# The first MLP's float64 weight tiles: fetched ahead of the branch and narrowed by a queue through the prologue

## The chip, the cores and the metric

The kernel runs on one core of one Trainium2 chip. The time is the device time of one execution in microseconds (us), lower is better; the kernel before takes 721.33 us in the median of three runs (718.95 to 722.62). The core's engines each work through a queue of their own in order: TensorE (PE, with its weight loads as PEld), VectorE (DVE), ScalarE (ACT), GpSimd (POOL), and SyncE (SP), which here issues all DMA transfers.

## What is computed

Windowed attention with a few global columns feeds two MLPs, one after the other. Cut to what matters:

```python
# attention: q, k, v (2, 8, 768, 64); keep = global columns, or 0 <= row - col < n_local (96)
a = softmax(where(keep, q @ k.T / 8 + bias, -1e9))
x = (a @ v).transpose(0, 2, 1, 3).reshape(1536, 512)
# first MLP: w_in (512, 2048), w_out (2048, 512)
h = x @ w_in
x = (h * cos(h)) @ w_out
# second MLP: w_gate, w_val (512, 1536), w_out (1536, 512)
g = x @ w_gate
out = (g / (1 + exp(-g)) * (x @ w_val)) @ w_out
```

The weights arrive as float64 and are worked on as float32. Each float32 operand of a large product is split in a high and a low part, and three products (high-high, high-low, low-high) are added up.

## The kernel before

**The weights.** Each weight matrix is cut in tiles of 128 x 512 float64 values (512 KB): 16 of `w1i` and 16 of `w1o` for the first MLP, 36 for the second. `fetch` (L167) takes a staging buffer `st` from a pool of three, issues the transfer on SP (L174) and returns `narrow`, which turns the 64-bit words into float32 with three VectorE operations on 128 x 512 integers: L183 (mask and shift of the high word), L186 (sign and exponent) and L193 (bits of the low word). The text calls these three together a narrowing. The result `w` stays in SBUF for all blocks. A staging buffer is free for the third fetch after it only when its narrowing has read it.

**Before each use** a `w` is split: ACT rounds it to the high part (L206, `ws`), and DVE or POOL subtracts to get the low part (L210).

**The windowed path.** A flag computed from `n_global` and `n_local` picks a branch (L142, L1158); with the inputs given it is `windowed_path`. Its `prologue` (L972) does the attention of the first four tiles of 128 tokens in eight pairs of heads: scores on PE (L777, with a mask added by L789), maximum on DVE (L795, `mx`) and its negative (L799, `nm`), exponentials on ACT (L809, `sb`), the split of the probabilities on ACT (L861) and POOL or DVE (L862, `ph`), a transposing DMA on SP (L864, `pt<-ph`), the product with `v` (L890), and at the end of a tile its normalization (L903, `xn`), PE transposes (L220), and the split into `xh` on ACT (L225) and `xl` on DVE (L226). Rows of `v` are also summed in absolute value for a scale (`va` L662, `vsum` L663, `vm` L669 to `vsc` L679).

**The first MLP.** `first_mlp` (L246) goes over three blocks of 512 tokens, 16 steps each. Step s of a block makes `h` with 12 matmuls (L274), then k on ACT (L300), f on DVE (L311), sine and square on ACT (L320, L321), the product on DVE (L328), its split (L332 on ACT, L338 on DVE), and two steps later 12 matmuls into `y` (L350). The other eight attention tiles are worked into the steps of the first two blocks: tile by tile at the steps of `BASES`, with scores L753 and their masked maximum on DVE (L829). In the last block the code is in the order in which it is written; up to there a scheduler orders each engine's queue ahead of time. All narrowings of the first MLP lie in its first block: step s asks for `w1i` tile s+2 and `w1o` tile s+1 at its start and narrows `w1i` s+2 and `w1o` s behind its chain:

```python
            if s < NF1:
                get("i", s + 2)
                get("o", s + 1)
...
            if s < NF1:
                use("i", w_in, s + 2)
                use("o", w_out, s)
```

Only `begin` (called at pair 5 of the prologue) narrows ahead of the steps: `w1i` 0 and 1.

Of the kernel before, what the change touches and what calls it, by code (L numbers as in the profile page):

```python
# [15 lines left out]
I32 = mybir.dt.int32  # L16
# [6 lines left out]
P = 128  # L23
B, H, S, D = 2, 8, 768, 64
NTOK = B * S
DM = H * D
# [31 lines left out]
HB = 5  # L58
HE = 6
GVE = "DMMDDDDDDMDM"  # L60
M1E = "GDDGGDG"
# [8 lines left out]
def attention_moe_moe2_kernel(  # L70
# [15 lines left out]
    NF1 = w1i.shape[0]  # L86
# [9 lines left out]
    ws_p = ctx.enter_context(tc.tile_pool(name="ws", bufs=2))  # L96
    st_p = ctx.enter_context(tc.tile_pool(name="st", bufs=3))

# [68 lines left out]
    def fetch(src, j, pool=wr_p, tag="w"):  # L167

        if not wide:
            w = pool.tile([P, DM], F32, tag=tag, name="w")  # L170
            nc.sync.dma_start(out=w, in_=src[j])
            return lambda half=None: w
        t = st_p.tile([P, DM, 2], I32, tag="st", name="st")
        nc.sync.dma_start(out=t, in_=src[j].bitcast(I32).rearrange("p (n w) -> p n w", w=2))  # L174
# [23 lines left out]

        return narrow

    def eng(which, n):
        return nc.vector if n < len(which) and which[n] == "D" else nc.gpsimd
# [20 lines left out]
    def x_split(i, xT):  # L223
        cols = slice(i * P, (i + 1) * P)
        nc.scalar.copy(out=xh[:, :, cols], in_=xT)  # L225
        nc.vector.tensor_tensor(  # L226
            out=xl[:, :, cols], in0=xT, in1=f32(xh[:, :, cols]), op=ALU.subtract
        )
# [17 lines left out]
    def first_mlp(c1, before, steps, last_block):  # L246
        w_in, w_out = {}, {}
        got = {}
        todo = [(b, j) for b in range(len(BLOCKS)) for j in range(NF1)]
# [3 lines left out]

        def get(nm, j):
            if j < NF1 and (nm, j) not in got:
                got[nm, j] = fetch(w1i if nm == "i" else w1o, j)

        def use(nm, d, j):
            if j < NF1 and j not in d:
                d[j] = got.pop((nm, j))()  # L260

# [103 lines left out]
        def begin():  # L365
            get("i", 0)
            get("i", 1)
            get("o", 0)
            use("i", w_in, 0)
            use("i", w_in, 1)  # L370
            prep_in(0)

        before(hp, begin, prep_in, h_early)
        ch_p = c1.enter_context(tc.tile_pool(name="ch", bufs=2))
# [3 lines left out]
        for s in range(last):  # L378
            early, late = steps.get(s, ((), ()))
            if s < NF1:  # L380
                get("i", s + 2)
                get("o", s + 1)
            ps = h_mm(s)
            if s >= 2:
                y_mm(s - 2)
            prep_in(s + 1)
            if s >= 1:
                chain_b(s - 1)
            for th in early:
                th()  # L390
            if s >= 1:
                chain_c(s - 1)
                chain_d(s - 1)
            if s < NF1:
                use("i", w_in, s + 2)
                use("o", w_out, s)
            prep_out(s - 1)
            chain_a(s, ps)
            for th in late:
                th()  # L400
# [186 lines left out]
    def windowed_path():  # L587
# [7 lines left out]
        with ExitStack() as ca:  # L595
# [375 lines left out]

            def prologue(hp, begin, prep_in, h_early):  # L972
                with (
# [33 lines left out]
                    for w in range(NW + LAG + 2):  # L1007
# [24 lines left out]
                        if w >= 1 and w - 1 < NW:  # L1032
                            i, pp = pairs[w - 1]
                            for p in (2 * pp, 2 * pp + 1):
                                pools["p"] = (pph, ph_p)[pp]
                                split_p(i, p, eng(PLE, 4 * i + p), nc.scalar.copy)
                        if w == HB:
                            begin()
# [22 lines left out]
    def general_path():  # L1061
        half = TB // 2 * P
        with ExitStack() as cg:
# [19 lines left out]
            for b in range(B):  # L1083
# [6 lines left out]
                for t in range(TB):  # L1090
# [63 lines left out]
                    nc.vector.tensor_copy(out=xn, in_=x)  # L1154
                    x_split(i, x_turn(xn, ps_x, "xT"))
        moe(lambda hp, begin, *_: begin(), {}, lambda: None)

# [46 lines left out]
```

## Time and profile before

| | before |
|---|---|
| median of 3 runs | 721.33 us |
| profiled execution | 719.88 us, span 718.1 us |
| PE busy | 668.2 us (93%) |
| DVE busy | 484.5 us (67%) |
| ACT busy | 390.0 us (54%) |
| POOL busy | 112.3 us (16%) |
| TensorE clock granted, mean | 0.958 |

The profile is of one execution, taken by the hardware profiler. Its span is 1.8 us shorter than that execution's own time, and this execution is 1.45 us faster than the median of the runs. Shares of busy time are averages over stages that differ: the prologue, the first block with the narrowings, the second block, and the rest. PE's busy time is that of modelled ends, and it counts half-clock work at its length, so a busy PE is not PE at its peak. The clock column is the granted share of full speed; the two levels are 1.2 and 2.4 GHz.

### The profile page before, as it was taken

How to read it: one execution, taken by the hardware profiler on the slowest of the kernel's cores; microseconds unless marked ns; L12 is line 12 of the kernel's file. 1: busy time of each engine (PE TensorE's matmuls, PEld its weight loads, DVE VectorE, ACT ScalarE, POOL GpSimd, SP SyncE). 2: the span in 40 equal slices, each digit the busy share in tenths (PEclk: the TensorE clock that was granted, in tenths of full speed). 3: DMA queues.
4: the chain of work that ended last, by engine and by line, in shares of the span. 5: the costliest groups of instructions: out<-in, count | busy, mean ns of one | idle time of the engine just before them, and what ended most of it. 6: DMA issues, size and time to landing. Idle time of an engine off the chain costs nothing.

```text
span 718.1 us, 9055 instructions
## 1 busy us (share of the span) xinstructions
PE 668.2 (93%) x3276; PEld 525.9 (73%) x3276; DVE 484.5 (67%) x885; ACT 390.0 (54%) x816; POOL 112.3 (16%) x108
## 2 busy tenths in 40 slices
PE   4767986997998999999999999999999999999996
PEld 2446764775776777787888888888888888888884
DVE  3897899799988565747999779887544443434441
ACT  4675757578497887766666643333343333333331
POOL 2663323423222332420000000000000000000000
PEclk9776899798999999999999999999999999999998
DMA  6799656657552222300322224532100000100001
GB/s 216 184 205 230 166 138 206 137 152 193 147 117 60 40 40 45 60 1 30 112 93 89 88 59 135 158 118 88 38 22 0 1 1 0 59 0 1 1 0 63
DMA packets 69508, 62.73 MB, mean 87 GB/s; under 512 B 48880, under 2 KB 55024, under 8 KB 69456
## 3 DMA queue, kind: packets, MB, share of 16 engines
q1 hardware_dynamic: 69456, 62.08, 31.8%
q8 instruction: 27, 0.44, 0.3%
q14 instruction: 25, 0.20, 0.1%
HBM read 47.19 MB, written 3.15 MB: 70 GB/s over the span
## 4 chain that ended last, share of the span: by engine, by line
PE 77%; DVE 11%; DMA 6%; ACT 3%; issue 1%; POOL 0%; SPq 0%; DVEq 0%; ACTq 0%; POOLq 0%
PE h L274 15%; PE v L492 14%; PE g L492 14%; PE o L528 14%; PE y L350 14%; PE s L753 3%; DMA st<-w1i 2%; DVE w L186 2%; PE x L890 1%; PE s L777 1%; DVE w L193 1%; DMA pt<-ph 1%; DVE w L183 1%; DMA v<-v 1%; DVE h L328 1%
## 5 line engine op out<-in xcount | busy, mean ns | idle before, releaser
L210 DVE TENSOR_TENSOR ws<-w,ws 128x512 fp32r<-128x512 f32 x161 | 111.2, 711 | 93.8 <-ACT ws L206 93.6
L350 PE MATMUL y<-g,ws 128*128 128x512 f32 x576 | 145.1, 397 | 12.6 <-ACT g L332 11.0
L274 PE MATMUL h<-xh,ws 128*128 128x512 f32 (+1 forms) x392 | 137.4, 411 | 2.7 <-ACT xh L225 2.5
L350 PEld LDWEIGHTS y<-g,ws 128*128 128x128 f32 x576 | 108.6, 191 | 39.1 <-ACT g L332 12.9
L206 ACT CAST ws<-w 128x512 fp32r<-128x512 f32 x204 | 121.8, 616 | 21.8 <-DVE w L193 16.8
L528 PE MATMUL o<-ws,a 128*128 128x512 f32 x432 | 104.7, 391 | 0.0
L492 PE MATMUL v<-xh,ws 128*128 128x512 f32 x288 | 96.3, 395 | 0.0
L274 PEld LDWEIGHTS h<-xh,ws 128*128 128x128 f32 x392 | 77.9, 201 | 24.1 <-ACT xh L225 3.2
L492 PE MATMUL g<-xh,ws 128*128 128x512 f32 x288 | 94.7, 390 | 0.0
L528 PEld LDWEIGHTS o<-ws,a 128*128 128x128 f32 x432 | 81.1, 188 | 18.4
L274 PE MATMUL h<-xl,ws 128*128 128x512 f32 (+1 forms) x196 | 79.7, 407 | 3.3 <-DVE xl L226 3.3
L210 POOL TENSOR_TENSOR ws<-w,ws 128x512 fp32r<-128x512 f32 x43 | 58.6, 1363 | 134.6 <-ACT ws L206 126.6
L504 ACT ACTIVATE sl<-g 128x512 f32<-128x512 f32 x36 | 21.5, 598 | 97.5 <-PE g L492 97.5
L492 PEld LDWEIGHTS v<-xh,ws 128*128 128x128 f32 x288 | 54.2, 188 | 12.7
L492 PEld LDWEIGHTS g<-xh,ws 128*128 128x128 f32 x288 | 54.1, 188 | 11.2
L514 ACT CAST a<-sl 128x512 fp32r<-128x512 f32 x36 | 22.4, 623 | 72.5 <-DVE sl L510 72.5
L492 PE MATMUL v<-xl,ws 128*128 128x512 f32 x144 | 56.9, 395 | 0.0
L492 PE MATMUL g<-xl,ws 128*128 128x512 f32 x144 | 56.0, 389 | 0.0
L186 DVE SCALAR_TENSOR_TENSOR w<-st,w 128x512 int32<-128x512 int32 x68 | 51.0, 760 | 1.2
L193 DVE SCALAR_TENSOR_TENSOR w<-st,w 128x512 int32<-128x512 int32 x68 | 50.2, 746 | 0.8
L300 ACT ACTIVATE k<-h 128x512 int32<-128x512 f32 x48 | 28.5, 594 | 39.3 <-PE h L274 39.2
L274 PEld LDWEIGHTS h<-xl,ws 128*128 128x128 f32 x196 | 39.4, 201 | 12.4 <-DVE xl L226 4.0
(109 smaller groups left out, 822.2 us busy)
## 6 DMA issues: line engine op xcount, KB each, us to landing
st<-w1i SPq DMA_DIRECT2D x16, 512.0 KB, 3.9
st<-w1o SPq DMA_DIRECT2D x16, 512.0 KB, 4.4
st<-w2g SPq DMA_DIRECT2D x12, 512.0 KB, 3.8
st<-w2v SPq DMA_DIRECT2D x12, 512.0 KB, 3.7
st<-w2o SPq DMA_DIRECT2D x12, 512.0 KB, 3.8
vr<-v SPq DMA_DIRECT2D x16, 256.0 KB, 3.8
kr<-kT SPq DMA_DIRECT2D x12, 256.0 KB, 3.8
qr<-qT SPq DMA_DIRECT2D x12, 256.0 KB, 3.7
```

The lines of the kernel that those rows point to most:

```text
L186: nc.vector.scalar_tensor_tensor(out=w, in0=hi, scalar=-(1 << 30), in1=w, op0=ALU.bitwise_and, op1=ALU.bitwise_or,)
L193: nc.vector.scalar_tensor_tensor(out=w, in0=lo, scalar=29, in1=w, op0=ALU.logical_shift_right, op1=ALU.bitwise_or,)
L206: nc.scalar.copy(out=s[:, 0, :], in_=w)
L210: e.tensor_tensor(out=s[:, 1, :], in0=w, in1=f32(s[:, 0, :]), op=ALU.subtract)
L274: nc.tensor.matmul(hps[s][:, c0:c1], lhsT=wis[s][:, a, k * P:(k + 1) * P], rhs=xx[:, k, t0 + c0:t0 + c1], start=(k == 0 and a == 0 and xx ...
L300: nc.scalar.activation(out=k[:, :n], in_=ps[:, :n], func=AF.Copy, scale=INV2PI)
L350: nc.tensor.matmul(ys[b][m][:, :n], lhsT=w[:, a, m * P:(m + 1) * P], rhs=g[:, c, :n], start=(j == 0 and a == 0 and c == 0), stop=(j == NF1 ...
L492: nc.tensor.matmul(ps[:, :n], lhsT=w[:, a, k * P:(k + 1) * P], rhs=xx[:, k, t0:t0 + n], start=(k == 0 and a == 0 and xx is xh), stop=(k == ...
L504: nc.scalar.activation(out=sl[:, :n], in_=ps_.pop(("g", s))[:, :n], func=AF.Silu)
L514: nc.scalar.copy(out=a[:, 0, :n], in_=sl[:, :n])
L528: nc.tensor.matmul(os_[b][m], lhsT=a[:, c, m * P:(m + 1) * P], rhs=w[:, d, :], start=(j == 0 and c == 0 and d == 0), stop=(j == NF2 - 1 an ...
L753: nc.tensor.matmul(o, lhsT=qr[r, i % 3, c, :], rhs=k, start=True, stop=True)
```

## The change

The three staging buffers become one tile of three slots, `st[:, n % 3]`. An `order` list holds the 32 tiles as they will be narrowed (i0, i1, i2, o0, i3, o1, i4, o2, and so on), and `fetch_next` issues the next. Three are fetched before the branch. `conv1` narrows the oldest tile fetched and fetches one more. The prologue calls it at each of its rounds as often as `CV` says, 13 times in all; each step of the first block calls it twice more while tiles are left; `need` calls it for whatever a step lacks. The branch not taken fetches its own again.

```diff
+CV = (2, 2, 1, 1, 1, 1, 1, 1, 1, 1, 1)
...
-    st_p = ctx.enter_context(tc.tile_pool(name="st", bufs=3))
+    st_p = ctx.enter_context(tc.tile_pool(name="st", bufs=1))
+    st = st_p.tile([P, 3, DM, 2], I32, name="st")
+    taken = [0]
...
-        t = st_p.tile([P, DM, 2], I32, tag="st", name="st")
+        t = st[:, taken[0] % 3]
+        taken[0] += 1
...
+    order = [t for j in range(NF1 + 2) for t in (("i", j), ("o", j - 2)) if 0 <= t[1] < NF1]
+    every = list(order)
+    fetched = []
+
+    def fetch_next():
+        if order:
+            nm, j = order.pop(0)
+            fetched.append(((nm, j), fetch(w1i if nm == "i" else w1o, j)))
+
+    for _ in range(3):
+        fetch_next()
...
-        def get(nm, j):
-            if j < NF1 and (nm, j) not in got:
-                got[nm, j] = fetch(w1i if nm == "i" else w1o, j)
-
-        def use(nm, d, j):
-            if j < NF1 and j not in d:
-                d[j] = got.pop((nm, j))()
+        def conv1():
+
+            if fetched:
+                (nm, j), fn = fetched.pop(0)
+                (w_in if nm == "i" else w_out)[j] = fn()
+                fetch_next()
+
+        def need(s):
+
+            while (s + 2 < NF1 and s + 2 not in w_in) or (s < NF1 and s not in w_out):
+                conv1()
...
-            get("i", 0)
-            get("i", 1)
-            get("o", 0)
-            use("i", w_in, 0)
-            use("i", w_in, 1)
+            while 1 not in w_in:
+                conv1()
             prep_in(0)
...
-            if s < NF1:
-                get("i", s + 2)
-                get("o", s + 1)
...
-                use("i", w_in, s + 2)
-                use("o", w_out, s)
+                conv1()
+                conv1()
+                need(s)
...
+                        for _ in range(CV[w] if w < len(CV) else 0):
+                            conv1()
```

The lines of the kernel move down with it: the narrowing is L187, L190 and L197, the fetch L178, the prologue's `mx` L810, f L331. What the scheduler makes of it is seen at three places.

SP's queue at the start of the program, from the load of the first keys (`kr`) and queries (`qr`) through the flag and the branch to the first rows of `v`. Before:

```order
L110 DMA kr<-kT 128x4x128
L115 DMA qr<-qT 128x512
L142 TENSOR_LOAD flag_i
L142 ISA x2
L1158 COMPARE_AND_BRANCH
L110 DMA kr<-kT 128x4x128
L115 DMA qr<-qT 128x512
L998 DMA v_223<-v 128x2x512
```

With the change:

```order
L113 DMA kr<-kT 128x4x128
L118 DMA qr<-qT 128x512
L178 DMA st<-w1i 128x1024
L145 TENSOR_LOAD flag_i
L145 ISA x2
L178 DMA st<-w1i 128x1024 x2
L1179 COMPARE_AND_BRANCH
L113 DMA kr<-kT 128x4x128
L118 DMA qr<-qT 128x512
L1013 DMA v_227<-v 128x2x512
```

Two fetches now stand between the flag and the second load of keys, and a third ahead of the flag.

DVE's queue in the prologue, from the end of the first tile's sums (`r<-sum`) past the maxima of the second tile's two halves (`mx`). Before:

```order
L897 TENSOR_SCALAR r<-sum 128x8
L900 RECIPROCAL r<-r 128x8
L862 TENSOR_TENSOR ph<-sb,ph 128x256
L795 TENSOR_REDUCE mx<-s_313 128x4
L799 TENSOR_SCALAR nm<-mx 128x4
L183 TENSOR_SCALAR w<-st 128x512
L795 TENSOR_REDUCE mx<-s_368 128x4
L669 TENSOR_REDUCE vm<-vsum 128x8
L799 TENSOR_SCALAR nm<-mx 128x4
L186 SCALAR_TENSOR_TENSOR w<-st,w 128x512
L673 TENSOR_SCALAR vm<-vm 128x8
```

With the change:

```order
L912 TENSOR_SCALAR r<-sum 128x8
L915 RECIPROCAL r<-r 128x8
L877 TENSOR_TENSOR ph<-sb,ph 128x256
L810 TENSOR_REDUCE mx<-s_337 128x4
L187 TENSOR_SCALAR w<-st 128x512
L814 TENSOR_SCALAR nm<-mx 128x4
L190 SCALAR_TENSOR_TENSOR w<-st,w 128x512
L197 SCALAR_TENSOR_TENSOR w<-st,w 128x512
L187 TENSOR_SCALAR w<-st 128x512
L810 TENSOR_REDUCE mx<-s_397 128x4
L684 TENSOR_REDUCE vm<-vsum 128x8
L190 SCALAR_TENSOR_TENSOR w<-st,w 128x512
```

These are the fourth and fifth narrowings in the changed queue; three more stand ahead of the piece, where before there were none. Up to the f of step 0 the queue has 15 whole narrowings and one operation of the next (before: four and three operations), from there to the f of step 8 the rest of 32 (before: up to the 20th).

DVE's queue in the first MLP, from the f of step 8 to the f of step 9. Before:

```order
L311 SCALAR_TENSOR_TENSOR f<-h,k 128x512
L338 TENSOR_TENSOR g<-h,g 128x512
L183 TENSOR_SCALAR w<-st 128x512 x2
L186 SCALAR_TENSOR_TENSOR w<-st,w 128x512 x2
L193 SCALAR_TENSOR_TENSOR w<-st,w 128x512 x2
L903 TENSOR_TENSOR xn<-x,r 128x512
L210 TENSOR_TENSOR ws<-w,ws 128x512
L328 SCALAR_TENSOR_TENSOR h<-f,h 128x512
L311 SCALAR_TENSOR_TENSOR f<-h,k 128x512
```

With the change:

```order
L331 SCALAR_TENSOR_TENSOR f<-h,k 128x512
L918 TENSOR_TENSOR xn<-x,r 128x512
L358 TENSOR_TENSOR g<-h,g 128x512
L734 CAST vs<-vr 128x512
L912 TENSOR_SCALAR r<-sum 128x8
L915 RECIPROCAL r<-r 128x8
L916 TENSOR_TENSOR r<-r,vsc_143 128x8
L735 TENSOR_TENSOR vs<-vr,vs 128x512
L227 TENSOR_TENSOR ws<-w,ws 128x512
L348 SCALAR_TENSOR_TENSOR h<-f,h 128x512
L331 SCALAR_TENSOR_TENSOR f<-h,k 128x512
```

No narrowing of the first MLP is left there; the rows of attention (`vs`, `r`) have moved up.

## Rows read from the trace of the kernel before

**Rows 1.** The page's slices: 40 equal parts of the span, busy tenths, granted clock.

```profile
PE   4767986997998999999999999999999999999996
PEclk9776899798999999999999999999999999999998
```

**Rows 2.** Windows, four stages: busy us (instructions) per engine, clock, DMA share, GB/s.

```profile
0.00:72.80 72.80, 47.93 (x331) 31.56 (x332) 50.13 (x99) 42.99 (x134) 32.55 (x46) 0.80 0.83 207
72.80:144.10 71.30, 61.93 (x284) 45.68 (x282) 63.10 (x133) 47.23 (x101) 25.67 (x19) 0.87 0.58 164
144.10:211.40 67.30, 62.19 (x348) 47.54 (x347) 62.74 (x126) 49.88 (x115) 20.53 (x17) 0.95 0.56 157
211.40:274.00 62.60, 60.63 (x337) 45.24 (x336) 44.82 (x106) 51.03 (x110) 19.48 (x16) 1.00 0.29 53
```

**Rows 3.** Timeline, DVE: the f of steps 0 and 24.

```profile
72.77 0.69 DVE L311 SCALAR_TENSOR_TENSOR f<-h,k 128x512 f32<-128x512 f32 x1 [1.10 <-ACT k L300]
...
273.96 0.68 DVE L311 SCALAR_TENSOR_TENSOR f<-h,k 128x512 f32<-128x512 f32 x1
```

**Rows 4.** Windows of DVE work on `st` alone (the narrowings): busy us, instructions.

```profile
20.00:72.80 52.80, 8.23 (x15) 0.73 0.93 211
72.80:144.10 71.30, 31.57 (x45) 0.87 0.58 164
144.10:211.40 67.30, 27.29 (x36) 0.95 0.56 157
```

**Rows 5.** The chain that ended last, 0 to 110 us: start, us, what.

```profile
7.46 5.53 DMA v<-v
...
13.54 1.50 ACT sb L809 x8
...
43.31 0.06 DVE mx L795
...
91.74 2.05 DVE w L186 x2
```

**Rows 6.** Timeline, SP's queue: issues between the branch and the rows of v.

```profile
6.20 0.56 SPq L110 DMA_DIRECT2D kr<-kT  x1
...
11.43 0.67 SPq L174 DMA_DIRECT2D st<-w1i  x1
...
64.33 0.38 SPq L174 DMA_DIRECT2D st<-w1o  x1
```

**Rows 7.** Windows, all engines: three stretches of the prologue.

```profile
6.00:20.00 14.00, 9.60 (x41) 5.73 (x43) 5.94 (x21) 8.26 (x33) 1.94 (x5) 1.00 0.70 243
20.00:72.80 52.80, 38.33 (x292) 25.83 (x291) 43.06 (x72) 33.00 (x100) 28.66 (x24) 0.73 0.93 211
13.00:17.00 4.00, 2.71 (x8) 1.11 (x8) 0.00 (x0) 3.59 (x16) 0.00 (x0) 1.00 1.05 401
```

**Rows 8.** Timeline, DVE: its two longest waits in the prologue.

```profile
18.09 0.17 DVE L897 TENSOR_SCALAR r<-sum 128x8 f32<-128x8 f32 x1 [6.28 <-ACT sb L809]
...
65.81 0.41 DVE L736 COPY vs<-relt 32x1024 f16<-32x1024 f16 x1 [3.26 <-PE x L890]
```

**Rows 9.** Timeline, DVE: two narrowings side by side.

```profile
82.38 0.76 DVE L183 TENSOR_SCALAR w<-st 128x512 int32<-128x512 int32 x2
...
83.76 1.29 DVE L186 SCALAR_TENSOR_TENSOR w<-st,w 128x512 int32<-128x512 int32 x2
84.97 1.29 DVE L193 SCALAR_TENSOR_TENSOR w<-st,w 128x512 int32<-128x512 int32 x2
```

**Rows 10.** Timeline, POOL and DVE: the same operations while POOL works.

```profile
88.07 3.05 POOL L210 TENSOR_TENSOR ws<-w,ws 128x512 fp32r<-128x512 f32 x2 [6.09 <-ACT ws L206]
...
89.88 1.86 DVE L183 TENSOR_SCALAR w<-st 128x512 int32<-128x512 int32 x2
91.66 2.13 DVE L186 SCALAR_TENSOR_TENSOR w<-st,w 128x512 int32<-128x512 int32 x2
```

**Rows 11.** Timeline, DVE: its longest wait from step 0 to 8.

```profile
138.27 0.29 DVE L829 CUSTOM_DVE_ANT_0 sb<-s,m 128x128 f32<-128x128 f32 x1 [3.18 <-PE s L753]
```

More of the change, by code (lines that the diff above doesn't have):

```diff
@@ L247, in first_mlp @@
         w_in, w_out = {}, {}
-        got = {}
         todo = [(b, j) for b in range(len(BLOCKS)) for j in range(NF1)]
@@ L365, in begin @@
         def begin():
-            get("i", 0)
-            get("i", 1)
-            get("o", 0)
-            use("i", w_in, 0)
-            use("i", w_in, 1)
+            while 1 not in w_in:
+                conv1()
             prep_in(0)
-        before(hp, begin, prep_in, h_early)
+        before(hp, begin, prep_in, h_early, conv1)
         ch_p = c1.enter_context(tc.tile_pool(name="ch", bufs=2))
@@ L970, in windowed_path, with prologue @@
             }
-            def prologue(hp, begin, prep_in, h_early):
+            def prologue(hp, begin, prep_in, h_early, conv1):
                 with (
@@ L1155, in general_path @@
                     x_split(i, x_turn(xn, ps_x, "xT"))
+        del fetched[:]
+        order[:] = every
+        for _ in range(3):
+            fetch_next()
         moe(lambda hp, begin, *_: begin(), {}, lambda: None)
```

## The prediction

> **What bounds the kernel now.** I read the slices of the page first [rows 1]. From the 18th slice on PE is busy nine tenths or more at full clock; before that PE and its clock go up and down together. So only the first 211 us or so can move. I cut the time at the f operation of steps 0, 8, 16 and 24 of the first MLP (the first and the last of the four in [rows 3]) and took busy times per stage [rows 2]. The reader is to see three different limits.
>
> Up to step 0 (72.8 us) nothing is full: DVE is busy 50.1 us, PE 47.9. From step 0 to 8 (71.3 us) DVE is busy 63.1 us; PE's 61.9 us are worth 61.9 x 0.87 = 53.9 us at full clock. From step 8 to 16 (67.3 us) DVE is busy 62.7 us, PE 62.2 at a clock of 0.95, so 59.1 at full clock. DVE bounds both stages, PE close behind in the second. Then step 16 to 24, with no narrowing, takes 62.6 us, PE busy 60.6 at full clock: PE bounds it. The narrowings [rows 4] are 8.2 us of DVE work after 20 us in the prologue, 31.6 us in steps 0 to 8 and 27.3 us in steps 8 to 16. The chain that ended last agrees: in the steps it runs through the w operations, and in the prologue through loads, exponentials and, for some ten us from 43 us on, DVE's queue [rows 5].
>
> **The change, part by part.** No narrowing and no transfer is saved: 32 tiles before and after. It is only their place that moves. By the order of the queues, up to step 0 there are 11 whole narrowings more, and two single operations fewer in balance; from step 0 to 8 there are 16 and two operations (before 14 and three); from step 8 on none (before 12).
>
> *Price of a narrowing.* Two of them side by side: L183 0.76 us for both, L186 from 83.76 to 84.97, L193 much the same [rows 9]: 0.38 + 0.60 + 0.60 = 1.6 us each, with nothing else on the way. In the prologue before they cost 8.23 / 5 = 1.65 us, in the steps 2.1 (31.57 / 15) and 2.3 (27.29 / 12) [rows 4].
>
> *Start.* The first three narrowings (4.8 us) fall where DVE waited 6.28 us for the first exponentials [rows 8]: they cost nothing. If that wait were gone they would cost their 4.8 us. Two fetches are issued between the flag and the loads of keys, queries and the first rows of v. The chain goes through that load of v: issued at 7.46, it took 5.53 us, and ACT's exponentials start at 13.54 behind it [rows 5]. An issue takes SP 0.6 us [rows 6], so the load is at least 1.2 us later. One MB at the 401 GB/s at which the queue moved from 13 to 17 us [rows 7] is 2.6 us. Ends: 1.2, and 3.8 if they add. I take 2.6, since the issues run while the data move. The fetch ahead of the flag costs nothing: SP stood waiting for the flag there, until 6.2 us.
>
> *Rest of the prologue.* Eight more narrowings less 1.0 us for the single operations: 8 x 1.6 - 1.0 = 11.8 us on DVE. From 20 to 72.8 us DVE was busy 43.06 [rows 7], so 9.7 us were free. The longest piece, 3.26 us before the copy at 65.81 [rows 8], waits on PE's x and the transposes behind it, and by the order two narrowings stand there: it takes 3.3 us of them. Of the other 6.4 us, all short gaps, I take half, 3.2: a narrowing in front of a maximum fills a gap, and delays the maximum that ACT waits for by as much. 11.8 - 3.3 - 3.2 = 5.3 us. Ends: 2.1 (all gaps filled) and 11.8 (none). Prologue together: 2.6 + 5.3 = +7.9 us (3.3 to 15.6).
>
> *Steps 0 to 8.* Two narrowings more, less one operation: +2.6 us of DVE work; rows of attention move both ways, -0.4 in balance. DVE's free time there is 8.2 us; 3.18 us of it stand behind PE's scores at 138.27 [rows 11], in the stage with the lower granted clock of the two with narrowings (0.87 against 0.95 [rows 2]). I choose to count this gap as gone, since PE should have its weights earlier and wait less: 2.6 - 0.4 - 3.2 = -1.0 us. Ends: +2.2 (waits as before), and -6.0 (8.2 us of waits gone).
>
> *Steps 8 to 16.* Without 27.3 us of narrowings DVE needs some 35 us and cannot bound the stage. What bounds then is PE, as in steps 16 to 24: 62.6 us [rows 2]. 67.3 - 62.6 = -4.7 us. Ends: 0 (the chain of k, f, sine, g hangs as before) and -8.2 (PE's 59.1 us at full clock without a gap).
>
> *After step 16* PE bounds on both sides; the second MLP's narrowings and fetches stay where they are. 0.
>
> Sum: 7.9 - 1.0 - 4.7 = +2.2 us. The profiled execution took 719.9 us, so 722.1; it is 1.45 us under the median of the runs, which makes 723.5 us. The point of it: DVE's free time ahead of step 0 is bought with delay of the prologue, while the stage relieved, steps 8 to 16, has PE close behind DVE and gives back only 4.7 of the 27.3 us taken out.
>
> A rule of the Trainium skill speaks on the price. The rows first: while POOL subtracted (88.07 to 91.1), two L183 took 1.86 us and the two L186 after them 2.13 us, against 0.76 and 1.29 alone [rows 9, 10]. The Trainium skill, "SBUF — State Buffer", section "Who interferes with whom", says that a VectorE instruction with two SBUF inputs contends with a GpSimd instruction that reads SBUF, and that the loser fully blocks; the trace agrees in the growth shown. By that rule the prologue, POOL's busiest stage, would be the worst place for narrowings; by the row of the prologue's own (1.65 us each) it is not. It gives the second rival.
>
> **The rivals.**
>
> *The prologue swallows it (faster).* All gaps filled, 3.3 us there, -1.0 in steps 0 to 8, and PE at full clock in steps 8 to 16, -8.2: -5.9 us, 714.0, or 715.4 by the median. For it: 22.7 us of DVE idle ahead of step 0, and PE at 0.95 of its clock in the stage relieved. Against: the chain runs through DVE's queue for part of the prologue, where more work delays the end at once. Chance 0.24.
>
> *DVE and POOL in each other's way (slower).* POOL is busy 28.66 of 52.8 us in the prologue [rows 7], 20.5 of 67.3 in steps 8 to 16 [rows 2]. Beside POOL a narrowing costs (1.86 + 2.13 + 2.13) / 2 = 3.1 us in place of 1.6. Eight of them at POOL's share of 54%: 8 x 0.54 x 1.5 = +6.5 us over the sum, 730 us. Against it stand the 1.65 us of the prologue's own five. It decides from about two in eight on: then the time passes 724.9. Chance 0.18.
>
> *The queue of SP and the DMA engines (slower).* From 20 us to step 0 there would be 11 fetches in place of 6 (7 up to 64.33 us, the first at 11.43 [rows 6]; 16 by the order, 5 of them early). Each now waits for a narrowing, and so do the transposes and the rows of v that stand behind it on SP. Five times 512 KB at 401 GB/s is 6.5 us; the DMA engines stood at 0.93 for 52.8 us [rows 7], so 3.7 us were free: +2.8 us, and with two such waits of 1.6 us on the chain +6.0: 726 to 729.5. Against: the share reads 1.05 in the row from 13 to 17 us, so it is no hard measure. Chance 0.18.
>
> That the change doesn't do what it says is excluded by the order of the queues.
>
> **How the numbers follow.** The likeliest case, 0.40, lies between 718 and 727. Faster and slower by over 0.5% is below 717.7 and above 724.9, about what a measurement of this kernel can tell from no change. Faster: 0.24, nearly all of the first rival. Slower: most of the other two (0.32 of 0.36) and 0.08 of the likeliest. Same: the remaining 0.36. The range for eight in ten reaches from near the first rival's time, 714.5, to past both slower ones, 731.5.
>
> **What the profile after would show.** The f of step 0 near 80.7 us (72.8 + 7.9), with DVE's idle before it down from 22.7 to about 14 us; the first exponentials near 16.1 us; the load of v longer than 5.53 us; step 8 near 151 and step 16 near 213.6 us; no narrowing behind step 8; PE's clock 1.00 from step 8 to 16. It is wrong upwards if the narrowings in the prologue average over 2 us or if the wait before the copy at the end of the prologue, 3.26 us before, does not shrink; it is wrong downwards if the f of step 0 comes before 77 us, or if steps 0 to 8 take less than 68 us because waits of PE behind narrowings counted for more than DVE's load.

## The result, and the profile after

The changed kernel takes 726.9 us (median; 722.8 to 733.3) against 720.5 us beside it on the same chip: 1.0103 times as long, 95% interval 1.0077 to 1.0129. It is slower by 1%. The profiled execution took 726.4 us, 6.5 more than that of the kernel before (719.9); all differences below are between these two. Stage times, here and for every kernel below, are those of the one execution that was profiled, and the executions of the changed kernel alone spread over 10 us.

The slices of the page, with PE's granted clock, against [rows 1]:

```profile
PE   3596789789999999999999999999999999999996
PEclk9956599689999999999999999999999999999999
```

The four stages again, cut at f of steps 0, 8, 16 and 24 (busy us and instructions of PE, PEld, DVE, ACT, POOL, then clock, DMA share, GB/s), against [rows 2]:

```profile
0.00:85.20 85.20, 54.93 (x335) 34.82 (x336) 67.20 (x131) 44.81 (x136) 35.09 (x47) 0.73 0.86 236
85.20:156.80 71.60, 62.07 (x319) 46.32 (x317) 63.30 (x137) 51.12 (x104) 23.82 (x18) 0.89 0.69 184
156.80:217.90 61.10, 58.49 (x303) 44.28 (x303) 36.87 (x91) 49.55 (x113) 19.77 (x18) 0.97 0.27 66
217.90:280.50 62.60, 61.14 (x340) 45.78 (x339) 44.63 (x105) 50.87 (x110) 19.44 (x16) 1.00 0.30 53
```

Read the second column downwards beside the same column of before: 72.8, 71.3, 67.3, 62.6 became 85.2, 71.6, 61.1, 62.6. The prologue lost 12.4 us, steps 8 to 16 gave back 6.2, and nothing else moved by more than 0.3. The prologue is where the question lies. DVE is busy 17.1 us more there, and its idle time went from 22.7 to 18.0 us (14 forecast). PE is busy 7.0 us more, with nearly the same matmuls (335 for 331), at a mean clock of 0.73 where it was 0.80.

The narrowings by stage (DVE work on `st` alone), against [rows 4]:

```profile
20.00:85.20 65.20, 25.30 (x37) 0.65 0.88 225
85.20:156.80 71.60, 33.70 (x50) 0.89 0.69 184
156.80:217.90 61.10, 0.00 (x0) 0.97 0.27 66
```

None is left behind step 8, as the change intends.

The chain up to the first cast of the scaled rows of v, against the first two rows of [rows 5] (start us, us, what):

```profile
8.63 6.63 DMA v<-v
...
15.82 1.50 ACT sb L824 x8
...
25.05 1.65 DVE w L197
...
28.76 0.63 DVE w L190
29.39 1.04 DVE vm L688
30.43 0.07 DVE nm L814
30.50 1.67 DVE w L197
...
34.26 1.26 DVE vs L734
```

The rows of v come later, and then the chain runs through narrowings (w) that stand between the small operations on vm, which have to be done before v can be scaled. PE shows what waited for that, and what it waited for later (timeline of PE; in brackets the idle time before the row and its releaser):

```profile
35.57 0.21 PE L905 MATMUL x<-vs,pt 128*128 128x64 f16 x1 [6.74 <-DVE vs L734]
...
69.20 0.66 PE L237 MATMUL xT<-ident,xn 128*128 128x128 f32 x4 [2.92 <-DVE xn L918]
...
72.54 2.68 PE L905 MATMUL x<-vs,pt 128*128 128x64 f16 x45 [2.60 <-DMA vs<-relt]
77.25 1.11 PE L237 MATMUL xT<-ident,xn 128*128 128x128 f32 x4 [2.03 <-DVE xn L918]
```

In the kernel before, the wait for the same small transfer was 1.61 us:

```profile
62.03 0.77 PE L890 MATMUL x<-vs,pt 128*128 128x64 f16 x21 [1.61 <-DMA vs<-relt]
```

So two halves of the prologue can be told apart, and I cut them at the row maxima of the fifth pair of scores, an operation that each of these kernels has: 34.77 us before, 40.02 after. The halves before, then after (columns as in the stages):

```profile
0.00:34.77 34.77, 20.63 (x95) 11.14 (x96) 19.97 (x47) 19.96 (x63) 13.96 (x31) 0.89 0.72 204
34.77:72.77 38.00, 27.27 (x240) 20.39 (x238) 30.14 (x52) 23.00 (x71) 18.59 (x16) 0.72 0.93 210
```

```profile
0.00:40.02 40.02, 18.75 (x89) 10.34 (x89) 29.02 (x60) 21.18 (x65) 18.28 (x33) 0.91 0.77 227
40.02:85.21 45.19, 36.19 (x247) 24.48 (x247) 38.19 (x74) 23.64 (x71) 16.82 (x15) 0.58 0.94 243
```

The first half is 5.2 us longer, and PE is idle in it for 21.3 us instead of 14.1. The second is 7.2 us longer, and there PE does not wait more: it is idle for 9.0 us (10.7 before) and busy for 36.2 (27.3 before), at a mean clock of 0.58 (0.72 before). By windows of 2 us the clock fell in the gap of 6.74 us, near 33 us, and rose again near 63.

### The profile page after: what moved, and what is told of

It is laid out like the page before. It is cut to its first block, busy times and chain, and to the rows that moved or that the text cites. A ratio compares the mean times of both kernels' runs of the same rounds, so it can differ in the third digit from the quotient of the medians.

```text
span 724.6 us, 9059 instructions
## 1 busy us (share of the span) xinstructions
PE 672.2 (93%) x3276; PEld 527.2 (73%) x3276; DVE 475.7 (66%) x885; ACT 395.0 (55%) x820; POOL 112.2 (15%) x108
## 3 DMA queue, kind: packets, MB, share of 16 engines
q1 hardware_dynamic: 69456, 62.08, 31.3%
## 4 chain that ended last, share of the span: by engine, by line
PE 77%; DVE 11%; ACT 5%; DMA 3%; issue 2%; POOL 1%; SPq 0%; ACTq 0%; DVEq 0%; POOLq 0%
PE h L294 14%; PE v L507 14%; PE g L507 14%; PE o L543 13%; PE y L370 13%; PE s L768 3%; PE s L792 2%; DVE w L197 2%; PE x L905 2%; DVE w L190 1%; DMA pt<-ph 1%; DVE w L187 1%; DMA v<-v 1%; ACT sb L862 1%; DVE h L348 1%
## 5 line engine op out<-in xcount | busy, mean ns | idle before, releaser
L294 PE MATMUL h<-xh,ws 128*128 128x512 f32 (+1 forms) x392 | 135.8, 409 | 3.0 <-DVE g L358 1.6
L370 PEld LDWEIGHTS y<-g,ws 128*128 128x128 f32 x576 | 108.3, 190 | 33.8 <-ACT g L352 8.0
L197 DVE SCALAR_TENSOR_TENSOR w<-st,w 128x512 int32<-128x512 int32 x68 | 51.1, 755 | 0.9
L190 DVE SCALAR_TENSOR_TENSOR w<-st,w 128x512 int32<-128x512 int32 x68 | 48.3, 714 | 1.4
L320 ACT ACTIVATE k<-h 128x512 int32<-128x512 f32 x48 | 28.5, 593 | 35.9 <-PE h L294 35.8
L348 DVE SCALAR_TENSOR_TENSOR h<-f,h 128x512 f32<-128x512 f32 x48 | 33.2, 692 | 22.2 <-ACT f L341 22.1
```

Source lines behind the costliest of these rows:

```text
L190: nc.vector.scalar_tensor_tensor(out=w, in0=hi, scalar=-(1 << 30), in1=w, op0=ALU.bitwise_and, op1=ALU.bitwise_or,)
L197: nc.vector.scalar_tensor_tensor(out=w, in0=lo, scalar=29, in1=w, op0=ALU.logical_shift_right, op1=ALU.bitwise_or,)
L294: nc.tensor.matmul(hps[s][:, c0:c1], lhsT=wis[s][:, a, k * P:(k + 1) * P], rhs=xx[:, k, t0 + c0:t0 + c1], start=(k == 0 and a == 0 and xx ...
L320: nc.scalar.activation(out=k[:, :n], in_=ps[:, :n], func=AF.Copy, scale=INV2PI)
L348: nc.vector.scalar_tensor_tensor(out=h[:, :n], in0=f[:, :n], scalar=0.5, in1=h[:, :n], op0=ALU.subtract, op1=ALU.mult,)
L370: nc.tensor.matmul(ys[b][m][:, :n], lhsT=w[:, a, m * P:(m + 1) * P], rhs=g[:, c, :n], start=(j == 0 and a == 0 and c == 0), stop=(j == NF1 ...
```

## The experiments

Four thoughts stood against each other: VectorE's queue is held up by the narrowings (the prediction's own term), the late load of v, the transfers (the prediction's third rival), and TensorE's clock, since the mean clock ahead of f of step 0 fell from 0.80 to 0.73. All ratios are to the kernel before on the same chip, with their 95% intervals; "the fifth maxima" is the cut above.

**Fetch two of the three tiles later.** Only one fetch stays ahead of the branch:

```diff
-    for _ in range(3):
+    for _ in range(1):
         fetch_next()
...
+                    for _ in range(2):
+                        fetch_next()
                     for w in range(NW + LAG + 2):
```

> The changed kernel, but only one of the three first fetches stands ahead of the branch; the other two are issued behind the prologue's first loads of v. Theory A (narrowings hold up DVE's queue by their own length): the first exponentials come some 2 us earlier, but two narrowings lose their place in DVE's first gap, so the f of step 0 moves by less than 2 us from its 85.2 us and the time stays at 725 to 727. Theory B (the late load of v is what costs): the f of step 0 comes at 81 us or before and the time is 723 or less.

728.3 us, 1.014 (1.010 to 1.018). The third maxima are back at 19.7 us (19.7 before, 21.9 after), but the fifth come at 41.9 and f of step 0 at 86.2. The late load is real and is not what decides: what it gives back is lost again behind it.

**No narrowing written in the rounds of the prologue; and three in round 0 alone.** Two kernels, `CV = ()` and `CV = (3,)`:

> The changed kernel without narrowings called for by the prologue's rounds (CV empty): the three fetches ahead of the branch stay, and the steps narrow two tiles each. By the order 8 to 9 narrowings remain ahead of the f of step 0. Theory A: the f of step 0 near 76 to 78 us, steps 8 to 16 between 62 and 67 us since they have narrowings again, time 719 to 723. Theory B: the f of step 0 no earlier than 82 us and a time of 725 or more, since the start is the same.

> The changed kernel with the prologue narrowing only the first three tiles, where DVE waits for the first exponentials. Theory A: those three are free, the rest is late enough: the f of step 0 near 76 to 78 us, time 718 to 722. Theory B: as the run without narrowings in the rounds, no earlier than 82 us, 725 or more.

728.8 us, 1.015 (1.011 to 1.020), and 728.5 us, 1.015 (1.010 to 1.019). Both missed their aim, for a reason the orders show: narrowings whose tiles are there are drawn forward, whatever the table says, and 9 and 10 of them still stand ahead of f of step 0 (15 in the changed kernel, 5 in the kernel before). f of step 0 came at 79.8 and 80.8, between what the two theories said (the profiled execution of the second kernel, 721.5 us, is 7 us quicker than its median). Fewer narrowings and fewer fetches, earlier f, but in the first of them 8 were left to steps 8 to 16, which then took 67.6 us again.

**A third of the narrowing.** The first 15 tiles get only the first of the three operations (work left out: the other two):

```diff
+        short = taken[0] < 15
...
-                nc.vector.scalar_tensor_tensor(
+                if not short:
+                    nc.vector.scalar_tensor_tensor(
...
+            if short:
+                return w.bitcast(F32)
```

> The changed kernel with work left out: the first 15 tiles are narrowed by the first of the three VectorE operations alone (their signs and low bits are lost), so that all fetches, waits and places in the queues stay and some 15 x 1.2 = 18 us of VectorE's time go. Theory A: the f of step 0 falls from 85.2 to 76 to 79 us and the time to 718 to 721. Theory B (loads, fetches and SP's waits cost): the f of step 0 stays above 82 us, the time above 723.

723.1 us, 1.007 (1.004 to 1.010), f of step 0 at 84.1. The first half is cured and the second is worse:

```profile
28.68 2.54 DVE L738 CAST vs<-v 128x512 f16<-128x512 f32 x2 [0.94 <-POOL v L730]
...
72.10 2.56 PE L909 MATMUL x<-vs,pt 128*128 128x64 f16 x45 [3.87 <-DMA vs<-relt]
```

The first row (DVE's timeline) is the cast that stood at 34.26 in the changed kernel and at 28.77 in the kernel before; the fifth maxima come at 34.4. The second row (PE's timeline) is the wait for a transfer that was 1.61 us before. Of the 49.7 us of this second half PE was busy 38.3, at a mean clock of 0.58. DVE was busy only 48.8 us ahead of f of step 0, less than in the kernel before, and the prologue was still 11.4 us longer. That felled the theory that VectorE's queue alone makes the loss.

**An eighth of the transfer; and both cuts together.** The first 15 tiles move 64 KB each, and the narrowings read that eighth eight times (work left out: seven eighths of these transfers; in the second kernel also two of the three operations):

```diff
+        m = 64 if taken[0] <= 15 else DM
...
-            hi, lo = t[:, :, 1], t[:, :, 0]
+            hi, lo = (
+                t[:, 0:m, a].unsqueeze(1).to_broadcast([P, DM // m, m]) for a in (1, 0)
+            )
```

> As the changed kernel, but each of its first 15 weight tiles moves an eighth of its bytes (64 KB for 512 KB) and the three narrowing operations read that eighth eight times over, so that VectorE does as much as in the changed kernel; work left out: seven eighths of those transfers, so the output is another. If the fetches crowd the DMA engines and SP's queue (rival 3 of the prediction), f of step 0 comes back from 85.2 us towards 76 to 78 and the ratio to the kernel before falls to 1.000 or lower. If the narrowings hold up VectorE's queue, the first cast of the scaled values stays at about 34 us (28.8 before) and f of step 0 at 83 to 86. If TensorE's half clock is the link between either and the end of the prologue, the half-clock time before f of step 0 follows f: about 30 us where f is at 76, 45 us where f is at 85.

> Both cuts at once: the first 15 tiles move an eighth of their bytes and are narrowed by the first operation only (work left out: seven eighths of those transfers and two of three narrowing operations; the output is another). If VectorE's queue and the DMA engines are the two costs, the prologue is at least as short as that of the kernel before: f of step 0 at 68 to 73 us, time 705 to 712 us with the gain of steps 8 to 16 kept. If the loss is in the rest of the change (the order of SP's queue, the late load of the values, the clock falling differently), f of step 0 stays at 79 us or later.

With small transfers alone 728.4 us, 1.011 (1.009 to 1.014): the first cast stands at 34.14 and the fifth maxima at 40.2, as in the changed kernel, but the second half takes 39.8 us where the changed kernel needs 45.2 (before: 38.0). It is the mirror of the run before it. f of step 0 came at 79.9, between what the two theories said, and the steps after it took longer than in the changed kernel (f of step 0 to f of step 16 140.4 us, not 132.7), which ate the gain; why is open. The half-clock time ahead of f of step 0 (2 x (1 - clock) x length, since the level is either full or half) was 2 x 0.27 x 79.9 = 43 us, against 46 in the changed kernel: over the whole prologue it hardly followed f, which had come forward by 5.3. With both cuts 720.1 us, 0.9997 (0.997 to 1.002), f of step 0 at 76.7. Neither cut alone brings f of step 0 below 79.9; both together take back 8.5 of the 12.4 us, less than I expected (68 to 73). The other 3.9 us stay without a cause: the first half is 38.2 us long, 3.4 longer than before, with a third of the narrowing work, small transfers and no late load. That the whole time equals that of the kernel before is in part chance of the later stages: steps 0 to 8 took 66.3 us, and steps 8 to 16 68.3 us at a clock of 0.90, without the gain of the change.

**Extra matmuls against the clock.** In the kernel before and in the changed one, two matmuls behind each probability split in rounds 1 to 5, into a PSUM tile that nobody reads:

```diff
+    if w in (1, 2, 3, 4, 5):
...
+        for _ in range(2):
+            nc.tensor.matmul(
+                T["warm"][:, 0:n], lhsT=fl[:, 0:P], rhs=fl,
+                start=True, stop=True,
+            )
```

> The kernel before with two extra matmuls behind each probability split of the prologue's rounds 1 to 5, whose results nobody reads, so that TensorE has fewer idle gaps. If the clock is what those gaps cost, the half-clock time before f of step 0 falls from 28.8 us to under 15 and f of step 0 from 72.8 us to 66 to 69, time 712 to 715 us. If TensorE waits for VectorE and the DMAs there anyway, f of step 0 stays at 72 to 74 whatever the clock does; if the extra matmuls only fill up a TensorE at half clock, f is later than 75.

> The changed kernel with the same extra matmuls. If the half clock carries most of its loss, half-clock time falls from 45.7 us to under 20, f of step 0 from 85.2 us to 73 to 77, and the ratio to the kernel before to 0.995 or lower. If VectorE's queue or the DMA engines carry it, f of step 0 stays above 82 with less half-clock time. If the extra matmuls lengthen a TensorE that is busy at half clock from 36 to 64 us, f is later than 86.

On the kernel before: 715.8 us, 0.996 (0.994 to 0.998), the only kernel here that beats both, by 0.4%; f of step 0 stayed at 73.2 and the gain came later (steps 0 to 8: 67.6 us, before 71.3). On the changed kernel: 728.3 us, 1.009 (1.005 to 1.014). Its two halves (columns as above):

```profile
0.00:41.37 41.37, 20.95 (x108) 11.38 (x108) 30.34 (x59) 20.35 (x64) 20.97 (x35) 0.89 0.73 225
41.37:85.08 43.71, 33.77 (x248) 22.61 (x249) 37.27 (x73) 24.27 (x72) 14.35 (x13) 0.70 1.03 244
```

The clock of the second half rose from 0.58 to 0.70 (half-clock time 2 x 0.42 x 45.2 = 38 us to 2 x 0.30 x 43.7 = 26 us), and f of step 0 came at 85.08 in place of 85.21. So 12 us less at half clock bought nothing. But the extra matmuls themselves kept PE busy for 3.7 us in the first half and 3.0 in the second; the second half became 1.5 us shorter and the first 1.3 us longer. The run shows that this remedy does not pay, not that the clock costs nothing.

**Each cost by itself, added to the kernel before.** One kernel gets 11 narrowings more in the prologue, made from a constant, with no transfer; the other 16 transfers more of 256 KB, with no narrowing:

```diff
+                        for _ in range(CV[w] if w < len(CV) else 0):
+                            n = len(early)
+                            narrow_more(n % 2 == 0, NF1 - 1 - n // 2)
```

```diff
+                        if 1 <= w <= 8:
+                            for x in (True, False):
+                                early[x, w + 7] = wr_p.tile([P, DM], I32, tag="w", name="w")
+                                nc.sync.dma_start(
+                                    out=early[x, w + 7],
+                                    in_=(w1i if x else w1o)[w].bitcast(I32)[:, 0:DM],
+                                )
```

> The kernel before with 11 extra narrowings in the prologue, two in each of the rounds 0 and 1 and one in each of the rounds 2 to 8, made from a constant that is there from the start, so that no transfer is added; their tiles are written again by the real narrowings later. By the two-cost theory VectorE's share of the loss shows in the first half of the prologue: the fifth row maxima (34.8 us in the kernel before, 40.0 in the changed one) come at 38 to 41, and what follows up to f of step 0 stays near the 38.0 us of the kernel before, so f of step 0 stands at 76 to 79 and the time at 722 to 726 us. If the narrowings alone make the loss, f of step 0 stands at 83 or later. If it is the transfers alone, f of step 0 stays at 72 to 74.

> The kernel before with 16 extra transfers of 256 KB of weights in the rounds 1 to 8 of the prologue, two in each, into tiles that the real narrowings write again later; no narrowing is added. By the two-cost theory the share of the transfers shows in the second half of the prologue: the fifth row maxima stay at 35 to 37 us, and from there to f of step 0 it takes 43 to 49 us instead of 38.0, so f of step 0 stands at 79 to 85 and the time at 724 to 731 us. If only VectorE's queue counts, f of step 0 stays at 72 to 74 and the time at 719 to 721 us.

The narrowings: 725.1 us, 1.008 (1.005 to 1.010), f of step 0 at 75.9, 3.1 us later than before. The fifth maxima came at 36.1, 1.3 us later and short of the 38 to 41 that I expected, though six of these narrowings stand ahead of them, as in the changed kernel. The transfers: 733.7 us, 1.017 (1.013 to 1.020), more than I expected, f of step 0 at 80.6, 7.9 us later. The halves of the first (36.08 and 39.82 us long), then of the second:

```profile
0.00:36.08 36.08, 20.17 (x97) 11.44 (x99) 27.67 (x59) 20.23 (x63) 17.09 (x32) 0.88 0.77 204
36.08:75.90 39.82, 28.38 (x237) 20.27 (x234) 38.83 (x70) 22.43 (x71) 19.87 (x15) 0.72 0.76 171
```

```profile
0.00:30.50 30.50, 16.20 (x69) 8.83 (x70) 15.97 (x43) 17.81 (x60) 10.45 (x29) 1.00 0.67 201
30.50:80.64 50.14, 36.17 (x267) 25.71 (x267) 31.91 (x55) 26.55 (x75) 21.47 (x18) 0.64 1.04 240
```

DVE is busy no more than before in the second kernel (47.9 us ahead of f of step 0, before 50.1), and yet its second half is the longest but one here. (Its fifth maxima come 4.3 us early, with no narrowing and 26 matmuls fewer in front of them, so f of step 0 is the safer number.) The views of its transfers (KB each, median us from issue to landing) and of PE's waits say a part of how:

```profile
kr<-kT SPq DMA_DIRECT2D x2, 256.0 KB, 5.3
pt<-ph SPq DMA_TRANSPOSE x14, 4.8
vs<-relt SPq DMA_DIRECT2D x2, 64.0 KB, 5.2
```

```profile
68.35 2.81 PE L894 MATMUL x<-vs,pt 128*128 128x64 f16 x45 [3.32 <-DMA vs<-relt]
```

In the kernel before, the same medians in its second half are 3.4, 3.6 and 2.6 us. The small transfers that the attention waits for land late. But PE's wait is only 1.7 us longer than the 1.61 before; of the 7.9 us, 4.5 are PE's busy time (52.4 us ahead of f of step 0, before 47.9), the rest its idle time. 3.1 + 7.9 = 11.0 us comes near the 12.4, as a sum of two loads that are not quite those of the changed kernel, nor in its order. This kernel lost 4.9 us more between f of step 0 and f of step 16 (143.6 in place of 138.7), which I can't explain.

**Fetch from round 3 on, with and without the extra matmuls.** No fetch ahead of the branch, and `CV = (0, 0, 0, 1, 1, 1, 1, 1, 1, 1, 1)`:

```diff
+                        if w == 3:
+                            for _ in range(3):
+                                fetch_next()
                         for _ in range(CV[w] if w < len(CV) else 0):
```

> The changed kernel with no fetch ahead of the branch, the first three fetches in round 3 of the prologue, and one narrowing in each round from 3 on: 10 tiles are narrowed by f of step 0 instead of 15. By the two-cost theory the first half is that of the kernel before (fifth row maxima at 34 to 36 us) and the second half is dearer than before by 3 to 6 us, so f of step 0 stands at 76 to 79; steps 8 to 16 still take 61 to 63 us, and the time is 714 to 720 us, ratio 0.993 to 1.000. If the loss is in the order of SP's queue or in the clock alone, f of step 0 stays at 80 to 86 and the ratio at 1.005 to 1.015.

> The kernel of the run before this one with the extra matmuls of the warm kernels in rounds 1 to 5. In the kernel before they brought 0.4%, in the changed kernel nothing. If they help where TensorE's waits are short, as in the kernel before, they bring 2 to 4 us here as well: 711 to 716 us, ratio 0.989 to 0.995, half clock under 30 us ahead of f of step 0. If VectorE and the transfers still set the prologue's end, the time is that of the run before within 2 us.

723.3 us, 1.006 (1.003 to 1.008). The prologue did as expected: fifth maxima at 34.6 as before, second half 43.9, f of step 0 at 78.5. The time missed: with 10 tiles narrowed by then instead of 15, steps 8 to 16 kept five narrowings and took 63.7 us, and steps 0 to 8 took 72.8 at a clock of 0.84. With the extra matmuls 727.8 us, 1.010 (1.006 to 1.014): the opposite of what I expected, second half 50.6 us. So of the three kernels that got these matmuls only the kernel before gained, 0.4%.

All second halves side by side. The bytes are the stretch's length times its GB/s; they are set by the edit in the small-transfer and more-transfer kernels, while elsewhere a longer stretch also lets more in:

| kernel | fifth maxima, us | from there to f of step 0, us | moved in it, MB | PE busy in it, us | PE clock | f of step 0, us |
|---|---|---|---|---|---|---|
| small transfers | 40.2 | 39.8 | 6.1 | 30.1 | 0.63 | 79.9 |
| before + narrowings | 36.1 | 39.8 | 6.8 | 28.4 | 0.72 | 75.9 |
| before | 34.8 | 38.0 | 8.0 | 27.3 | 0.72 | 72.8 |
| both cuts | 38.2 | 38.5 | 8.3 | 28.0 | 0.69 | 76.7 |
| `CV = ()` | 37.4 | 42.4 | 8.5 | 34.8 | 0.60 | 79.8 |
| before + matmuls | 34.6 | 38.6 | 8.6 | 28.0 | 0.77 | 73.2 |
| `CV = (3,)` | 36.9 | 43.9 | 9.3 | 32.8 | 0.67 | 80.8 |
| fetch from round 3 | 34.6 | 43.9 | 10.5 | 29.9 | 0.69 | 78.5 |
| the same + matmuls | 35.0 | 50.6 | 10.6 | 40.6 | 0.60 | 85.5 |
| changed + matmuls | 41.4 | 43.7 | 10.7 | 33.8 | 0.70 | 85.1 |
| changed | 40.0 | 45.2 | 11.0 | 36.2 | 0.58 | 85.2 |
| fetch two later | 41.9 | 44.3 | 11.4 | 35.7 | 0.58 | 86.2 |
| before + transfers | 30.5 | 50.1 | 12.0 | 36.2 | 0.64 | 80.6 |
| one operation | 34.4 | 49.7 | 12.1 | 38.3 | 0.58 | 84.1 |

Up to 8.6 MB the second half takes 38.0 to 39.8 us, with one exception; from 9.3 MB on, 43.7 to 50.6. That does not settle it for the bytes. `CV = ()` and the last kernel with matmuls moved no more in a second than the kernel before (200 and 209 GB/s, before 210) and took 42.4 and 50.6 us. And half-clock time sorts the column as well: up to 23.9 us of it the second half takes 38.0 to 39.8 us, from 26.2 us on 42.4 to 50.6, again with one exception (small transfers, 29.4 us). PE's idle time, the length less its busy time, sorts nothing: it is 7.6 to 14.0 us throughout. So a longer second half is for the most part PE busy for longer, and this table cannot tell whether bytes or clock come first, since a longer stretch has room for more of both.

## Why the prediction was right in its sign and too small in its size

The sum was to be 7.9 - 1.0 - 4.7 = +2.2 us; it was 12.4 + 0.3 - 6.2 = +6.5. The step that failed is *rest of the prologue*, +5.3 us in the prediction, 10.1 measured (12.4 - 2.3), still within the ends given for it (2.1 to 11.8). It was worked out from DVE's free time alone, with nothing for the transfers and nothing for PE's clock. The misses of the two later stages, +1.3 and -1.5 us, cancel by chance, so the whole miss is the prologue's.

- *Start*, +2.6: the load of v was issued at 8.63 and took 6.63 us, and the exponentials began at 15.82, 2.3 us later than before. Right; and the kernels with one early fetch or small ones had their third maxima back at 19.7 and 20.1 us.
- *Rest of the prologue, as a load on DVE's queue.* The first half is 5.2 us longer; without the start, 2.9. Cutting the narrowings to a third removed it all (34.4 us), so they have a part in it. How much of it is theirs by length is not shown: the same number of narrowings added to the kernel before cost 1.3 us there, and with both cuts the first half still took 38.2. It came in an order the prediction did not look at: pieces of narrowing between the operations on vm, ahead of the first cast, with PE idle for 6.74 us. The price was low as well. The narrowings in the prologue averaged 31.3 / 15.3 = 2.04 us, not 1.6, past the 2 us that the prediction named as the sign of an error upwards. The last operation of a narrowing (L197), twice on the chain above with 1.65 and 1.67 us, cost 0.68 us at most other places; those two ran beside POOL at work on a weight split (timeline of POOL):

```profile
24.49 1.65 POOL L227 TENSOR_TENSOR ws<-w,ws 128x512 fp32r<-128x512 f32 x1
...
30.36 1.26 POOL L227 TENSOR_TENSOR ws<-w,ws 128x512 fp32r<-128x512 f32 x1
```

  That is the second rival's mechanism in its place: 2 x 1 us. The three splits on POOL ahead of step 0 had come forward with their weights, to 24.5, 30.4 and 35.2 us from 35.9, 48.1 and 58.9. No run here tells it apart from the rest of the queue. One fits it: the narrowings added to the kernel before, whose tiles are not split on POOL, cost less in the first half. In the Trainium skill it is the rule of "SBUF — State Buffer", section "Who interferes with whom", that the prediction weighed; the trace agrees for these two operations.
- *Rest of the prologue, as a load on SP's queue and the DMA engines.* The term held nothing for this; it was the third rival, at a chance of 0.18 and 726 to 729.5 us. The second half is 7.2 us longer. Added alone to the kernel before, transfers cost 7.9 us ahead of f of step 0; taken alone from the changed kernel, the second half shrank by 5.4. So they have a part in it, but the rival's mechanism, waits for transfers on the chain, does not show: in this half PE waited 3.3 us for transfers before (1.61 of them in the row above) and 2.60 us in the changed kernel. In the changed kernel SP's own timeline (start, duration) shows a fetch in front of the small transfer that PE waited 2.60 us for:

```profile
68.05 0.54 SPq L178 DMA_DIRECT2D st<-w1i  x1
68.69 0.58 SPq L749 DMA_DIRECT2D vs<-relt  x1
```

  and its transfers of the second half, ten fetches where there were four, against the same view of the kernel before (second fence):

```profile
st<-w1i SPq DMA_DIRECT2D x5, 512.0 KB, 4.2
st<-w1o SPq DMA_DIRECT2D x5, 512.0 KB, 4.9
...
kr<-kT SPq DMA_DIRECT2D x2, 256.0 KB, 4.7
```

```profile
st<-w1i SPq DMA_DIRECT2D x2, 512.0 KB, 4.8
st<-w1o SPq DMA_DIRECT2D x2, 512.0 KB, 5.3
kr<-kT SPq DMA_DIRECT2D x2, 256.0 KB, 3.4
```

  How much is the queue's order and how much the engines' load was not told apart. Nor does the chain of the changed kernel itself run through a transfer there: from 35 to 64 us it names mostly PE at half clock, from 65 to 74 us DVE with narrowings in it. That the transfers matter is shown by adding and removing them; by what way they lengthen this half is not shown.
- *PE's clock ahead of step 0.* The sum had no term for it, though the prediction saw PE and its clock go up and down together. PE's busy time grew by 7.0 of the 12.4 us (-1.9 in the first half, +8.9 in the second), with 335 matmuls for 331. The clock fell near 33 us, in the gap of 6.74 us, and came back near 63; in the kernel before it fell near 27 us, in a gap of 2.56 us, and was back at 40.6. Narrowings and transfers may both work by way of the clock: with small transfers its mean in the second half was 0.63 and not 0.58, with both cuts 0.69. No run changed the clock without adding matmuls, so this rival is not excluded.
- *The gap of 3.26 us before the copy* [rows 8] is gone, as predicted; the copy at 75.22 follows the operation before it at once. That gap was filled, and the end came later all the same.
- *Steps 0 to 8*, -1.0: +0.3. I had counted DVE's wait for the scores [rows 11] as gone. It stands there as before:

```profile
147.09 0.29 DVE L844 CUSTOM_DVE_ANT_0 sb<-s,m 128x128 f32<-128x128 f32 x1 [3.13 <-PE s L768]
```

- *Steps 8 to 16*, -4.7: -6.2. PE bounds the stage, 58.5 of 61.1 us busy, as predicted, though its clock was 0.97 and not 1.00. One reason that the size came out larger is work that I had not counted: the stage holds 303 of PE's matmuls in place of 348. The 8 scores and 38 products with v that are gone from it (3.2 us) fall into other stages, 36 of the products into steps 0 to 8.

What stays open: why PE's clock is lower in the second half of most kernels with more transfers, how much of the second half is the clock and how much the transfers, the 3.9 us that stay with both cuts, and what the steps behind the prologue lost in the kernels with small and with added transfers.

## What to carry to other kernels

Work moved ahead in time brings its transfers along: price the bytes that the earlier stage must then carry beside the small transfers on the same queue, and not only the instructions on the engine that had idle time. Idle time in a stage that no engine fills can be latency of a chain, as it was here; a filler hurts where it comes between two links of it, so look at which links it will stand between. Split a stage's added length into PE's idle time and PE's busy time before naming its cause: 7.0 of the 12.4 us here were PE busy for longer at half clock, which no list of waits shows. And when cutting one of two costs changes nothing, cut both before calling it innocent.

## What the runs showed of the hardware that was not expected

TensorE kept half clock through 20 us with hardly a gap in the changed kernel, while in the kernel before it had full clock back at 40.6 us, after a stretch that was as full (windows of the one, then of the other; the third column is PE's busy time, the clock stands third from the end):

```profile
36.00:56.00 20.00, 19.89 (x110) 10.88 (x109) 16.79 (x29) 11.80 (x35) 9.56 (x8) 0.50 0.97 232
```

```profile
32.00:40.00 8.00, 8.00 (x51) 5.14 (x52) 7.97 (x12) 3.64 (x12) 5.43 (x5) 0.50 0.73 174
```

I have no cause for that. And an operation on 128x8 values took 1.11 us in the changed kernel and 0.17 us in the kernel with added narrowings (timelines of DVE and POOL, of the one, then of the other):

```profile
29.31 1.11 DVE L688 TENSOR_SCALAR vm<-vm 128x8 f32<-128x8 f32 x1
...
27.68 2.71 POOL L877 TENSOR_TENSOR ph<-sb,ph 128x512 f16<-128x512 f32 x2 [1.54 <-ACT ph L876]
```

```profile
24.98 0.17 DVE L693 TENSOR_SCALAR vm<-vm 128x8 f32<-128x8 f32 x1
...
25.59 2.79 POOL L882 TENSOR_TENSOR ph<-sb,ph 128x512 f16<-128x512 f32 x2 [3.29 <-ACT ph L881]
```

In the first POOL was subtracting until 30.39 us, when the small operation ended; in the second POOL stood idle until 25.59. So even an operation on eight values a partition can cost the chain a microsecond beside POOL.
